# First fixed tiles of three experts take their split weights from SBUF, in 64-row pair products; tile loads cut at 256 rows; another order of the work

## The chip, the cores and the metric

The kernel runs on one core of one Trainium2 chip. The core's engines are named as the profile names them: PE is TensorE (matmuls; PEld is its weight load, which overlaps them), DVE is VectorE, ACT is ScalarE, POOL is GpSimd and SP is SyncE, which here issues nearly all DMA transfers. The metric is the time of one execution on the device in microseconds (us), as the median of several runs; less is better.

## The reference

Eight sequences of 3584 tokens with 192 features go through a causal convolution over seven tokens, whose taps are a softmax per token and head (eight heads of 24 features). Each of the 28672 results then goes to the one expert of eight with the highest gate logit: a relu layer of 1024 features and a layer back to 192, times the gate probability and a sigmoid.

```python
def _attn_ref(x, weight_gen):                      # x (8, 3584, 192), weight_gen (8, 3584, 8, 7)
    w = np.exp(weight_gen - np.max(weight_gen, axis=-1, keepdims=True))
    w = w / (np.sum(w, axis=-1, keepdims=True) + 1e-09)
    x_pad = np.concatenate([np.zeros((B, K - 1, D), dtype=np.float32), x], axis=1)
    idx = np.arange(S)[:, None] + np.arange(K)[None, :]
    x_unf = x_pad[:, idx, :].reshape(B, S, K, H, group)
    return np.einsum('bshk,bskhg->bshg', w, x_unf).reshape(B, S, D)

def _moe_ref(x, w_gate, w_output_gate, w1, w2):    # x (28672, 192)
    logits = x @ w_gate
    e_idx = np.argmax(logits, axis=1)
    probs = np.exp(logits - logits.max(-1, keepdims=True))
    probs /= probs.sum(-1, keepdims=True) + 1e-09
    gate_w = probs[np.arange(N), e_idx]
    eom = 1.0 / (1.0 + np.exp(-(x @ w_output_gate)))
    for e in range(E):
        mask = e_idx == e
        h = np.maximum(x[mask] @ w1[e], 0.0)
        out[mask] = gate_w[mask, None] * eom[mask, e, None] * (h @ w2[e])
```

## The kernel before

**Units.** The tokens are worked in 32 units of 896. For each, softmax taps are made and multiplied with shifted rows of x: some products by POOL (`gap`), the others by DVE (`vap`). For units 0 to 6 (`u < PE_U`) PE adds the seven products, as matmuls with an identity; from unit 7 on DVE adds them in PSUM (`acc_steps`). A unit's rows are then split into two 16-bit parts and laid in a row buffer `rt` (three of them, `RT`), turned, put through the gate matmul, ranked by expert, and scattered, sorted by expert, to DRAM (`srtd`) by seven indirect DMAs of POOL. A row buffer is free again when its unit's seven scatters have landed, so unit u+3's split waits for unit u's scatters. Units 0 to 6 are turned on PE (through PSUM and `gt`), the later ones by transposing DMAs that SP issues.

**Weights.** `weight_steps` stages each expert's w1 and w2 in SBUF (`st`), and `split_steps` scales them (by the sum of squares that ACT takes first) and splits them into high and low 16-bit halves, `wa` for w1 and `wpb` for w2. SP stores both to DRAM (`wd`), and the buffers go back to the pool.

**Tiles.** A tile is up to 512 rows of one expert. `plan_rounds` says how many tiles of which size are made after which unit. After unit 2 come eight fixed tiles of 256 rows, one per expert (`EACH`, made by `each_table`); later rounds choose the experts with the most waiting rows (`round_table`), and the last round takes the rest. For a tile, SP loads its rows' gate values (`meta`), its rows with a transposing DMA (`xT` or `xTb`, two buffers in turn), and its weights (`wa`, `wb`) from `wd`; `tile_steps` keeps two tiles ahead (`AHEAD`, `LATE`). The rows have 192 features in two parts, so three blocks of 128 partitions; the middle one holds 64 rows of each part. ACT copies its first 64 rows to a tile `dup` whose other half is zero (`twin_steps`). The first layer, `gemm1_unit`, then makes five products per 128 features of the hidden layer: three with blocks 0 and 2, and two with the middle block and `dup`. `gemm1_twins` is another form, for up to four tiles of the last round that are 128 rows long: there products of 64 rows stand in pairs on the two halves of the array. ACT takes relu (`hh`), DVE the low part (`hl`), PE makes the second layer (`gemm2_group`, 24 products per 128 rows), ACT scales it (`ys`), and POOL scatters it to the output by an indirect DMA.

**What sets the order.** All five engines' instructions are recorded by a planner (`Order`, `Chain`, `Paced`, `Queue`) before the kernel is built. Each chain of steps has a rank (`RANK_*`, with exceptions in `RK` and `FAVOUR`); the planner has a cost for each operation and due times (`FIRST` for the start, `LATER` after it, `PACKET` and `TURN_NS` for DMAs), and at each step it takes the chain that may go first. An engine runs its list in order: an instruction that waits holds up all behind it. In the profile almost every operation therefore has the same line (165, or 140 for SP), and groups are told apart by their tiles' names. PSUM banks for tiles are given by `bank_steps`, not before unit 6 has been split:

```python
yield T_, lambda: (len(ahead) >= GIVE or "split" in U[PE_U - 1]) and any(f[1] == 0 for f in sum_free)
```

## Time and profile before

| what | value |
|---|---|
| median of three runs | 1207.81 us (1205.61 to 1212.14) |
| the profiled execution's own time | 1206.35 us |
| its span in the profile | 1204.6 us |
| PE busy | 1108.7 us, 92% of the span |
| DVE busy | 930.3 us, 77% |
| POOL busy | 833.3 us, 69% |
| ACT busy | 653.6 us, 54% |
| mean busy share of the 16 DMA engines, main queue | 68.2% |
| HBM | 174.87 MB read, 59.62 MB written |

The profile is of one execution. Its page gives the busy time of each engine; the views of its trace cut that by stretches of time, by tile and operation, by what an engine waited for, or show each operation in order of time. The idle time of an engine matters only where the end of the kernel hangs on it.

### The profile page before, as it was taken

Reading aid. Unit: us, or ns where it says so; the run is one execution under the profiler, and the core shown is the slowest. Engines: PE = TensorE matmul, PEld = TensorE weight load, DVE = VectorE, ACT = ScalarE, POOL = GpSimd, SP = SyncE. Lnnn points to the kernel's source line nnn. Section 1 sums busy time; section 2 is a strip of 40 time slices with the busy share of each in tenths; the row PEclk is TensorE's granted clock in tenths of the full one; section 3 lists DMA queues with packets and bytes.
Section 4 is the critical chain, followed back from the end, with each engine's and each line's share of the span. In section 5 each row is a group of like instructions: output and inputs, shape, how many; then the busy total and the mean of one; then the engine's idle time right before and its main releaser. Section 6 shows DMA issues by size and latency. Waiting matters only on the chain.

```text
span 1204.6 us, 27077 instructions
## 1 busy us (share of the span) xinstructions
PE 1108.7 (92%) x9707; PEld 806.5 (67%) x9707; DVE 930.3 (77%) x1776; ACT 653.6 (54%) x1418; POOL 833.3 (69%) x613
## 2 busy tenths in 40 slices
...
GB/s 275 189 215 222 267 245 270 248 255 288 250 240 179 253 228 179 197 280 207 188 259 238 214 220 157 237 219 187 214 204 209 159 208 288 286 215 336 279 302 44
DMA packets 269129, 275.56 MB, mean 229 GB/s; under 512 B 206918, under 2 KB 231479, under 8 KB 267968
## 3 DMA queue, kind: packets, MB, share of 16 engines
q1 hardware_dynamic: 247152, 229.21, 68.2%
...
HBM read 174.87 MB, written 59.62 MB: 195 GB/s over the span
## 4 chain that ended last, share of the span: by engine, by line
PE 40%; DVE 23%; DMA 16%; issue 8%; POOL 5%; SPq 5%; ACT 3%; DVEq 0%; POOLq 0%; ACTq 0%
PE ps L165 40%; DVE ps L165 11%; DMA srtd<-rt,posi 6%; SPq L140 5%; DVE hl L165 3%; DMA xTb<-srtd 3%; DMA xs<-in_x_dram 2%; DVE hlb L165 2%; POOL gap L165 2%; DVE vt L165 2%; DMA xT<-srtd 2%; POOL out_dram L165 2%; DVE rt L165 1%; POOL srtd L165 1%; DMA wa<-wd 1%
## 5 line engine op out<-in xcount | busy, mean ns | idle before, releaser
L165 POOL TENSOR_TENSOR gap<-xs,w 128x1344 f32<-128x1344 f32 x145 | 376.7, 2602 | 51.7 <-DVE ps L165 21.5
L165 PEld LDWEIGHTS <-wa 128*128 128x128 f16 (+1 forms) x2440 | 227.3, 98 | 205.4 <-issue 25.6
L165 POOL DMA_INDIRECT out_dram<-ys,meta x216 | 214.7, 994 | 211.6 <-ACT ys L165 165.4
L165 POOL DMA_INDIRECT srtd<-rt,posi x224 | 226.1, 1009 | 92.5 <-issue 59.8
L165 PE MATMUL ps<-wb,hh 128*128 128x192 f16 x1888 | 243.1, 246 | 3.4 <-ACT ys L165 2.7
L165 PE MATMUL ps<-xT,wa 128*128 128x512 f16 (+3 forms) x1056 | 224.5, 343 | 19.3 <-DMA wa<-wd 6.6
L165 PE MATMUL ps<-wb,hl 128*128 128x192 f16 x944 | 232.2, 246 | 0.0
L165 PE MATMUL ps<-wb,hhb 128*128 128x192 f16 x1760 | 227.5, 246 | 1.3 <-DVE hl L165 0.8
L165 DVE SCALAR_TENSOR_TENSOR hl<-ps,hh 128x512 f16<-128x512 f32 (+1 forms) x240 | 158.1, 672 | 83.6 <-ACT hh L165 83.2
L165 PE MATMUL ps<-wb,hlb 128*128 128x192 f16 x880 | 216.7, 246 | 0.0
L165 DVE SCALAR_TENSOR_TENSOR hlb<-ps,hhb 128x512 f16<-128x512 f32 (+1 forms) x226 | 146.6, 666 | 84.8 <-ACT hhb L165 84.3
L165 PE MATMUL ps<-xTb,wa 128*128 128x512 f16 (+3 forms) x928 | 203.6, 349 | 8.1 <-DMA wa<-wd 3.1
L165 ACT ACTIVATE ys<-ps,sc 128x192 f32<-128x192 f32 x228 | 96.0, 421 | 182.2 <-PE ps L165 115.9
L165 ACT ACTIVATE hh<-ps 128x512 f16<-128x512 f32 (+1 forms) x240 | 139.4, 589 | 88.2 <-PE ps L165 85.3
L165 PEld LDWEIGHTS <-hh 128*128 128x128 f16 x1888 | 170.9, 98 | 21.7 <-issue 4.2
L165 DVE TENSOR_TENSOR ps<-ps,gap 128x1344 f32<-128x1344 f32 x117 | 181.2, 1549 | 1.8 <-POOL gap L165 1.5
L165 PEld LDWEIGHTS <-hhb 128*128 128x128 f16 x1760 | 159.8, 98 | 20.7 <-issue 2.9
L165 ACT ACTIVATE hhb<-ps 128x512 f16<-128x512 f32 (+1 forms) x226 | 129.5, 585 | 77.2 <-PE ps L165 75.9
L165 PE MATMUL ps<-dup,wa 128*128 128x512 f16 (+5 forms) x456 | 155.9, 352 | 0.0
L165 PEld LDWEIGHTS <-hl 128*128 128x128 f16 x944 | 92.3, 98 | 0.0
L165 PEld LDWEIGHTS <-hlb 128*128 128x128 f16 x880 | 86.2, 98 | 0.0
L165 PE MATMUL ps<-gap,cf 128*128 128x512 f32 x168 | 73.9, 581 | 13.3 <-POOL gap L165 11.7
...
## 6 DMA issues: line engine op xcount, KB each, us to landing
...
```

Source lines behind the costliest of these rows:

```text
L140: r = f(*args, **kwargs)
L165: r = f(*args, **kwargs)
```

## The change

- **Weights where they lie.** For experts 5, 6 and 7 (`DIRECT`) the split halves `wa` and `wpb` stay in SBUF after they have been stored; the first fixed tile of each uses them, and its load reads only `meta` and rows. These buffers go back to the pool after that tile. Every other tile of these experts loads its weights as before.
- **Pair products.** In `wa` as it was split, the middle block's weights lie on both halves of the partitions (the first 512 hidden features on one, the others on the other). For the three tiles, `swap_steps` copies both halves of the middle block crosswise into a new tile `swap` (two buffers of 256 columns), and `gemm1_direct` makes the block's products as 64-row products in pairs, one on each half of the array: 24 of these beside 24 full ones.
- **Loads.** A tile's transposing load is cut at 256 rows (`TSPLIT`).
- **Copies.** The plan counts the copy to `dup` as possible 3.7 us later than the transposing load's end (`DUP_LAG`).
- **Order.** The fixed tiles come in the order 5, 6, 7, 0 to 4 (`EACH_ORDER`). `EARLY`, and with it the sizes of the rounds, changes: the round of unit 5 has one tile of 512 rows (before three of 384), that of unit 6 four of 384 (two), that of unit 7 none (one of 512), that of unit 8 two of 512 (one). In all there are 14 tiles of 256 rows, 4 of 384, 43 of 512 and 16 of 128 (before 13, 5, 43 and 15). `each_table` has tiles of its own per unit. `RK`, `FAVOUR`, `RANK_T` and the planner's costs have other numbers.

The numbers of products per engine for the sums of units 0 to 6 (`FRONT`, `PAIRS`) are written anew in the diff but come out as before; these lines are left out below.

```diff
@@ -247,7 +247,7 @@
 def sync_issue(name, args, kwargs):
-    return 1.2 if name == "dma_start_transpose" else 0.532
+    return 1.3 if name == "dma_start_transpose" else 0.532
@@ -274,6 +274,8 @@
     run = size * min(run_of(o), run_of(kwargs["in_"]))
+    if run == 4 * WA_W:
+        return n / run * 300.0 / 16e3
@@ -465,7 +467,8 @@
         dup_free.append(dup)
-    state = {"base": base, "writers": [], "t": 0, "weights": 0, "rounds": 0, "rows": 0, "stored": {}}
+    swap_free = [cp.tile([P, 256], F16, name=f"swap{i}") for i in range(2)]
+    state = {"base": base, "writers": [], "t": 0, "weights": 0, "rounds": 0, "rows": 0, "stored": {}, "here": {}, "used": set()}
@@ -601,7 +604,8 @@
         od.cur.t = max(od.cur.t, SP.moved + 1.0)
-        wa_free.append((od.cur.t, wa))
+        if e not in DIRECT:
+            wa_free.append((od.cur.t, wa))
@@ -611,9 +615,12 @@
         st_free.append(od.cur.t)
+        if e in DIRECT:
+            state["here"][e] = (od.cur.t, wa, wb)
...
         SP.dma_start(out=wd[e, :, WA_W:WW], in_=wb)
-        wb_free.append((od.cur.t, "wb"))
+        if e not in DIRECT:
+            wb_free.append((od.cur.t, "wb"))
@@ -1008,7 +1015,7 @@
         state["step"] = None
-        ge, to, ti = (sp.tile([1, NE], d, tag=k, bufs=1, name=f"{k}{u}") for k, d in (("ege", F32), ("eto", F32), ("eti", I32)))
+        ge, to, ti = (sp.tile([1, NE], d, tag=f"{k}{u}", bufs=1, name=f"{k}{u}") for k, d in (("ege", F32), ("eto", F32), ("eti", I32)))
@@ -1077,15 +1084,20 @@
+    def direct(e):
+        return e in DIRECT and e not in state["used"]
...
         while "all" not in state or queue:
-            yield SP, lambda: queue and dup_free and (state["weights"] == NE or queue[0][4] in state["stored"]) and len(ahead) < (LATE if "all" in state else AHEAD)
+            yield SP, lambda: queue and (direct(queue[0][4]) and swap_free or not direct(queue[0][4]) and dup_free and (state["weights"] == NE or queue[0][4] in state["stored"])) and len(ahead) < (LATE if "all" in state else AHEAD)
             _, xT = yield from take(xt_free, SP)
-            _, ka = yield from take(wa_free, SP)
-            _, kb = yield from take(wb_free, SP)
+            ka = kb = None
+            if not direct(queue[0][4]):
+                _, ka = yield from take(wa_free, SP)
+                _, kb = yield from take(wb_free, SP)
             T, ti, i, pads, fixed, ready = queue[0]
-            ready = max(ready, state["stored"].get(fixed, 0.0))
+            ready = max(ready, state["stored"].get(fixed, 0.0) if ka is not None else 0.0)
@@ -1095,6 +1107,8 @@
             d = tile_load(state["t"], T, ti, i, list(state["writers"]), ka, kb, xT, fixed)
+            if ka is None:
+                state["used"].add(fixed)
@@ -1107,13 +1121,19 @@
             e = bass.ds(nc.sync.snap(expert, min_val=0, max_val=NE - 1), 1)
-        else:
+        elif ka is not None:
...
         loaded(SP.dma_start(out=meta[:, 0:Gn, :], in_=rows[:, W - 2 : W].rearrange("(g p) c -> p g c", p=P)), writers)
-        loaded(SP.dma_start_transpose(out=xT[:, :, 0:T], in_=rows.bitcast(F16)[:, 0:384]), writers)
-        turned = od.cur.t
+        for lo in range(0, T, TSPLIT):
+            hi = min(T, lo + TSPLIT)
+            loaded(SP.dma_start_transpose(out=xT[:, :, lo:hi], in_=srtd[bass.ds(row + lo if lo else row, hi - lo), :].bitcast(F16)[:, 0:384]), writers)
+        turned = od.cur.t + DUP_LAG
+        if ka is None:
+            d = dict(t=t, T=T, G=Gn, units=8 // (512 // T), meta=meta, xT=xT, own=own, hh={}, hl={}, hl_t=0.0, dup=swap_free.pop(0), twin=None, h=[])
+            od.add(swap_steps(d), (RANK_H,), S, turned)
+            return d
@@ -1124,6 +1144,40 @@
         return d
+    def swap_steps(d):
+        xT, T = d["xT"], d["T"]
+        S.copy(d["dup"][64:128, 0:T], xT[0:64, 1, 0:T])
+        S.copy(d["dup"][0:64, 0:T], xT[64:128, 1, 0:T])
+        yield S, lambda: d["own"] in state["here"]
+        ready, ka, wb = state["here"].pop(d["own"])
+        d.update(ka=ka, kb="wb", wa=ka.bitcast(F16), wb=wb.bitcast(F16), inv=wb.bitcast(F32)[:, 1536:1537])
+        d["dup_t"] = max(od.cur.t, ready)
+    def gemm1_direct(d, u, banks):
+        T, wa, xT, dup = d["T"], d["wa"], d["xT"], d["dup"]
+        nf = 512 // T
+        us = [u + k * d["units"] // 2 for k in range(2)]
+        hs = d["h"][-2:]
+        def place(k, i):
+            return ps[:, banks[k] + i * T : banks[k] + (i + 1) * T]
+        for i in range(nf):
+            for q in range(3):
+                for k in range(2):
+                    p0, at = 64 * k, 2048 + (u * nf + i) * P + (512 if q == 2 else 0)
+                    rhs = xT[p0 : p0 + 64, 1, 0:T] if (q == 1) == (k == 1) else dup[p0 : p0 + 64, 0:T]
+                    T_.matmul(place(k, i), lhsT=wa[p0 : p0 + 64, at : at + P], rhs=rhs, start=(i == 0 and q == 0), stop=False, skip_group_check=True)
+        for k, at in enumerate(banks):
+            _, hh, hl = hs[k]
+            for i in range(nf):
+                f = (us[k] * nf + i) * P
+                for q, (wo, b) in enumerate(((f, 0), (1024 + f, 0), (f, 2))):
+                    T_.matmul(place(k, i), lhsT=wa[:, wo : wo + P], rhs=xT[:, b, 0:T], start=False, stop=(q == 2), skip_group_check=True)
+            od.add(evac_steps(d, ps[:, at : at + nf * T], hh[:, 0 : nf * T], hl[:, 0 : nf * T], at, us[k]), (RANK_H,), S, T_.t + od.m("LAT_P"), ("h", d["t"], us[k]))
@@ -1277,7 +1331,18 @@
                 moved = True
-            elif cur is not None and cur["twin"] is None and len(h_free) >= 2:
+            elif cur is not None and "own" in cur and len(h_free) >= 2:
+                yield T_, lambda: "dup_t" in cur
+                banks = []
+                for _ in range(2):
+                    _, at = yield from take(bank_free, T_)
+                    cur["h"].append((yield from take(h_free, T_)))
+                    banks.append(at)
+                od.cur.t = max(od.cur.t, cur["ready"], cur["dup_t"])
+                gemm1_direct(cur, i // 2, banks)
+                i += 2
+                moved = True
+            elif cur is not None and cur["twin"] is None and "own" not in cur and len(h_free) >= 2:
@@ -1290,7 +1355,7 @@
                     wa_free.append((od.cur.t, cur["ka"]))
-                    dup_free.append(cur["dup"])
+                    (swap_free if "own" in cur else dup_free).append(cur["dup"])
@@ -1401,17 +1466,20 @@
 RANK_S = 1.5
-RANK_T = 5
-TURN_NS = 30.0
+RANK_T = 3.5
+TURN_NS = 27.0
+TSPLIT = 256
+DUP_LAG = 3.7
...
-LATER = {'LAT': 0.125, 'LAT_S': 0.037, 'LAT_G': 0.04, 'LAT_P': 0.167, 'LAT_T': 2.466, 'LAT_R': 0.0, 'LOCK': True, 'SLACK': 0.0, 'LEAD': 5.44, 'WBX': 5.724}
-CONST_AT = 4.2
+LATER = {'LAT': 0.112, 'LAT_G': 0.009, 'LAT_P': 0.084, 'LAT_R': 0.0, 'LAT_S': 0.037, 'LAT_T': 2.401, 'LEAD': 5.44, 'LOCK': True, 'SLACK': 0.0, 'WBX': 5.724}
+CONST_AT = 2.2
 STG = 2
+DIRECT = (5, 6, 7)
@@ -1429,13 +1497,13 @@
 PRO_G = 4
...
-RK = {('b', 0): 1.2, ('b', 1): 1.5, ('b', 2): 1.2, ('b', 7): 5.5, ('c', 0): 1.2, ('c', 1): 1.2, ('e', 1): 1.2, ('e', 6): 4.8, ('g', 5): 1.5, ('l', 1): 4.2, ('l', 6): 1.5, ('r', 2): 1.2, ('r', 9): 4.8, ('s', 2): 1.5, ('x', 0): 6.5, ('x', 8): 6.5}
+RK = {('a', 9): 1.5, ('b', 4): 1.5, ('b', 9): 2.2, ('c', 4): 2.2, ('c', 5): 4.2, ('c', 7): 1.5, ('e', 4): 1.5, ('e', 6): 3.5, ('e', 8): 2.8, ('g', 4): 4.2, ('l', 2): 4.8, ('l', 3): 2.2, ('r', 9): 2.2, ('v', 0): 4.2, ('x', 8): 4.8, ('x', 9): 4.8}
...
 SHARES = {}
-FAVOUR = {('e', 8): -1.6, ('s', 1): 4.1}
+FAVOUR = {('e', 5): -1.4, ('h', 1, 0): 1.2, ('s', 1): 4.1, ('y', 2, 1): -2.6}
@@ -1443,12 +1511,13 @@
 DEFER = 6
...
 EACH = {2: (256,)}
-EACH_ORDER = tuple(range(8))
-EARLY = {2: ((256, 0),), 3: ((512, 0),), 5: ((384, 0),), 6: ((384, 0),)}
+EACH_ORDER = (5, 6, 7, 0, 1, 2, 3, 4)
+EARLY = {2: ((384, 0),), 3: ((384, 0),), 4: ((512, 0),), 6: ((384, 0),)}
```

How the lists of the engines move is shown at three places. Numbers behind a name tell buffers apart; the first number of `gap`, `posi` and `vap` is the unit.

POOL before, around the scatters of unit 3 (`posi3`), whose last one gives row buffer `rt_0` back for unit 6:

```order
L165 TENSOR_TENSOR gap6_3_1182<-xs1_84,w6_672 128x1344
L165 DMA srtd_78<-rt_0_99,posi3_1137 262144x194 x3
L165 TENSOR_TENSOR gap7_0_1241<-xs1_84,w7_849 128x1344
L165 DMA srtd_78<-rt_0_99,posi3_1137 262144x194
L165 TENSOR_TENSOR gap7_1_1266<-xs1_84,w7_849 128x1344
L165 DMA srtd_78<-rt_0_99,posi3_1137 262144x194
L165 TENSOR_TENSOR gap7_2_1315<-xs1_84,w7_849 128x1344
L165 DMA srtd_78<-rt_0_99,posi3_1137 262144x194 x2
L165 DMA srtd_78<-rt_1_100,posi4_1329 262144x194 x7
```

POOL after, at the same place:

```order
L165 TENSOR_TENSOR gap6_2_1244<-xs1_84,w6_746 128x1344
L165 DMA srtd_78<-rt_0_99,posi3_1124 262144x194 x2
L165 TENSOR_TENSOR gap6_3_1305<-xs1_84,w6_746 128x1344
L165 DMA srtd_78<-rt_0_99,posi3_1124 262144x194
L165 DMA srtd_78<-rt_1_100,posi4_1313 262144x194
L165 DMA srtd_78<-rt_0_99,posi3_1124 262144x194
L165 DMA srtd_78<-rt_1_100,posi4_1313 262144x194
L165 DMA srtd_78<-rt_0_99,posi3_1124 262144x194
L165 DMA srtd_78<-rt_1_100,posi4_1313 262144x194
L165 TENSOR_TENSOR gap7_0_1420<-xs1_84,w7_860 128x1344
```

The products of unit 7 (`gap7`) stood among the last scatters of unit 3; now they stand behind them, and scatters of unit 4 have come between unit 3's last three.

SP before, around the loads of the tiles numbered 1 and 2 (`meta1`, `xT1`, `meta2`); `wa0`, `wa1`, `wpb6` are the split weights of experts on their way to DRAM:

```order
L140 DMA meta1_1384<-srtd_78 128x2x2
L140 ISA
L140 DMA_TRANSPOSE xT1_168<-srtd_78 128x3x256
L140 DMA wa2_138<-wd_79 128x1536
L140 DMA wb1_1388<-wd_79 128x1537
L140 DMA wd_79<-wa1_137 128x1024
L140 DMA wd_79<-wa1_137 64x256 x4
L140 DMA wd_79<-wpb6_1479 128x1537
L140 TENSOR_LOAD eti2_877
L140 ISA x3
L140 DMA meta2_1606<-srtd_78 128x2x2
L140 ISA
```

SP after, around the load of tile 2:

```order
L140 DMA wd_79<-wa0_136 128x1024
L140 DMA wd_79<-wa0_136 64x256 x4
L140 DMA wd_79<-wpb6_1394 128x1537
L140 DMA wd_79<-wa1_137 128x1024
L140 DMA wd_79<-wa1_137 64x256 x4
L140 DMA wd_79<-wpb7_1523 128x1537
L140 TENSOR_LOAD eti2_850
L140 ISA x3
L140 DMA meta2_1650<-srtd_78 128x2x2
L140 ISA
L140 DMA_TRANSPOSE xTb0_1614<-srtd_78 128x3x256
L140 TENSOR_LOAD eti2_850
```

The load of tile 2 has no load of weights behind it now, and stands behind the stores of the last two experts' weights, where before only one store stood ahead of it; tile 1's load has gone further ahead.

DVE before, ahead of the split of unit 6 (the last row, `rt`); `cs`, `nx`, `z`, `ge`, `ti` belong to the table of a round:

```order
L165 SCALAR_TENSOR_TENSOR cs_127<-gg5_0_1433,ps_82 1x24
L165 TENSOR_REDUCE ps_82<-w9_1243 128x56
L165 SCALAR_TENSOR_TENSOR z5_0_1429<-cs_127,nx5_0_1428 1x8x3
L165 TENSOR_TENSOR ge5_0_1452<-cs_127,ps_82 1x27
L165 TENSOR_SCALAR ps_82<-ps_82 128x56
L165 SCALAR_TENSOR_TENSOR ps_82<-cs_127,z5_0_1429 1x8
L165 TENSOR_TENSOR ge5_0_1452<-ge5_0_1452,z5_0_1429 1x27
L165 RECIPROCAL ps_82<-ps_82 128x56
L165 TENSOR_REDUCE ti5_0_1461<-ge5_0_1452 1x3
L165 TENSOR_TENSOR w9_1243<-w9_1243,ps_82 128x56x5
L165 SCALAR_TENSOR_TENSOR rt_0_99<-ps_82,sx6_1435,rt_0_99 128x7x192
```

DVE after, ahead of the same split:

```order
L165 SCALAR_TENSOR_TENSOR ps_82<-cs_127,ps_82 1x8
L165 TENSOR_TENSOR ge5_0_1432<-ge5_0_1432,ps_82 1x9
L165 TENSOR_REDUCE ps_82<-lz5_1376 128x7
L165 TENSOR_TENSOR w9_1338<-w9_1338,ps_82 128x392
L165 TENSOR_REDUCE ti5_0_1444<-ge5_0_1432 1x1
L165 TENSOR_SCALAR ps_82<-ps_82 128x2
L165 TENSOR_SCALAR wsc7_1446<-ps_82 128x2
L165 TENSOR_SCALAR winv7_1447<-ps_82 128x2
L165 TENSOR_SCALAR ex_x6_1461<-ssq6_1439 128x1
L165 SCALAR_TENSOR_TENSOR ez5_1454<-ps_82,ez5_1454 128x7
L165 RECIPROCAL ez5_1454<-ez5_1454 128x7
L165 SCALAR_TENSOR_TENSOR rt_0_99<-ps_82,sx6_1459,rt_0_99 128x7x192
```

The table of unit 5's round is one of three tiles before (24 numbers, with `z` in SBUF) and of one tile after (8 numbers, with its result in PSUM); the scaling of the weights of expert 7 (`wsc7`) and the factors of unit 6 (`ex_x6`) stand ahead of the split now.

## Rows read from the trace of the kernel before

**Rows 1.** The page, busy time of each engine with its share and count of instructions

```profile
PE 1108.7 (92%) x9707; PEld 806.5 (67%) x9707; DVE 930.3 (77%) x1776; ACT 653.6 (54%) x1418; POOL 833.3 (69%) x613
```

**Rows 2.** Stretches: length, busy PE, PEld, DVE, ACT, POOL; PE's clock, DMA share, GB/s

```profile
161.00:180.00 19.00, 2.88 (x25) 2.67 (x25) 14.24 (x27) 8.46 (x17) 10.53 (x8) 0.50 0.64 205
180.00:260.00 80.00, 72.28 (x735) 64.91 (x734) 67.46 (x100) 46.62 (x103) 47.62 (x29) 0.95 0.93 260
260.00:980.00 720.00, 687.62 (x6038) 492.15 (x6036) 650.00 (x1274) 406.11 (x930) 582.42 (x429) 1.00 0.81 218
1100.00:1204.60 104.60, 96.82 (x1114) 82.17 (x1112) 30.43 (x44) 44.60 (x97) 24.48 (x25) 0.97 0.76 230
```

**Rows 3.** Waits of PE, by releaser: us in total, times, longest us

```profile
PE ps L165 <- DMA wa<-wd: 9.7, 6, 2.8
PE ps L165 <- ACT ys L165: 9.0, 10, 1.9
PE ps L165 <- DVE hl L165: 6.7, 12, 1.2
PE ps L165 <- DVE hlb L165: 6.2, 10, 2.2
```

**Rows 4.** Timeline, 145 to 181 us: start, us, engine, operation [idle before <- releaser]

```profile
145.69 1.48 ACT L165 ACTIVATE wa<-st 128x1536 bf16<-128x1536 f32 x1
...
157.99 0.98 POOL L165 DMA_INDIRECT srtd<-rt,posi  x1 [0.31 <-issue]
...
164.86 0.22 ACT L165 ACTIVATE rt<-tok 128x14 int32<-128x14 f32 x1 [6.06 <-DMA srtd<-rt,posi]
...
167.72 5.40 DVE L165 SCALAR_TENSOR_TENSOR z<-cs,nx 1x24 f32<-1x24 f32 x1
...
167.98 5.10 POOL L165 TENSOR_TENSOR gap<-xs,w 128x1344 f32<-128x1344 f32 x2
...
176.33 2.40 PE L165 MATMUL ps<-ident,rt 128*128 128x128 f16 x21 [14.94 <-DVE rt L165]
...
179.72 1.01 PE L165 MATMUL ps<-xT,wa 128*128 128x256 f16 x4 [0.99 <-ACT gt L165]
...
180.15 1.01 POOL L165 DMA_INDIRECT srtd<-rt,posi  x1 [7.08 <-ACT rt L165]
```

**Rows 5.** Timeline of SP's queue: the first load of tiles 2, 5 (rows), 14

```profile
185.33 0.42 SPq L140 DMA_DIRECT2D meta<-srtd  x1
...
219.77 1.25 SPq L140 DMA_TRANSPOSE xTb<-srtd  x1
...
321.79 0.39 SPq L140 DMA_DIRECT2D meta<-srtd  x1
```

**Rows 6.** Waits of all engines: ACT's copies, for one pair of buffers

```profile
ACT dup L165 <- DMA xTb<-srtd: 41.6, 22, 4.0
```

**Rows 7.** Timeline of PE, pair products of a tile of the last round

```profile
1053.93 0.38 PE L165 MATMUL ps<-dup,wa 64*128 64x512 f16 x1
1054.23 2.98 PE L165 MATMUL ps<-xTb,wa 128*128 128x512 f16 x13
```

**Rows 8.** Timelines of POOL, PE, DVE; then two groups by line (busy, mean ns)

```profile
191.51 1.01 POOL L165 DMA_INDIRECT srtd<-rt,posi  x1 [0.17 <-issue]
...
195.88 0.60 PE L165 MATMUL ps<-xT,wa 128*128 128x256 f16 x4
...
196.42 0.60 PE L165 MATMUL ps<-xT,wa 128*128 128x256 f16 x4
...
288.76 0.26 DVE L165 TENSOR_TENSOR_SCAN p<-segs,ps 128x56 f16<-128x56 f16 x1
...
320.48 1.03 PE L165 MATMUL ps<-xTb,wa 128*128 128x512 f16 x4
...
L165 DVE SCALAR_TENSOR_TENSOR hl<-ps,hh 128x512 f16<-128x512 f32 (+1 forms) x240 | 158.1, 672 | 83.6 <-ACT hh L165 83.2
...
L165 DVE TENSOR_TENSOR ps<-ps,gap 128x1344 f32<-128x1344 f32 x117 | 181.2, 1549 | 1.8 <-POOL gap L165 1.5
```

13 lines of the change are left out of this document (7 added, 6 removed).

## The prediction, made before the changed kernel had run

> **What bounds the kernel now.** I read the page's busy line first: TensorE (PE) is busy 1108.7 of 1204.6 us [rows 1], so it idles 95.9 us in all. The reader is to see that no other engine comes near that, and that a gain must be idle time of PE, or PE work, that goes away. The work hardly changes: the plan gives tiles of 512, 384, 256 and 128 rows in the numbers 43, 5, 13, 15 before and 43, 4, 14, 16 after, 29184 rows both times. So I read PE's idle time by stretch, as length less PE busy [rows 2]: 16.1 us in 161 to 180, 7.7 in 180 to 260, 32.4 in the 720 us from 260 to 980 and 7.8 after 1100; the rest, some 32 us, lies mostly before 161. Next the waits of PE [rows 3] say what ends those after the start: weights (wa) 9.7 us, ys 9.0, hl and hlb together 12.9. Last the timeline around the one large gap [rows 4], where the first tile is held.
>
> That gap reads as a chain. Unit 6 may not be split before unit 3's last scatter gives back its row buffer (there are three); ScalarE (ACT) waits 6.06 us for it until 164.86. Then VectorE (DVE) should finish the split (rt) at once, but ahead of it z, an operation on 24 numbers, takes 5.40 us, from 167.72, while GpSimd (POOL) runs two products, 167.98 to 173.08. PE waits 14.94 us for rt, turns unit 6 at 176.33 and begins tile 0 at 179.72. Tile 0 had been loaded long before: the first tile is held by unit 6, not by its rows or weights. The PSUM banks for tiles come free with that split (`bank_steps`).
>
> **The change part by part.** The sum stands against the profiled execution's own time, 1206.35 us (span 1204.6 and 1.75 around it); the median of the three runs, 1207.81, is 1.5 above.
>
> *Order at the start: -7.* POOL now has three products fewer and two scatters more ahead of unit 3's last scatter. At 2.55 us a product (5.10 for two) and about 1.3 a scatter (0.98 and the gap to the next) that is 7.7 - 2.6 = 5.1 us earlier: 164.86 becomes about 159.8. The round of unit 5 has one tile instead of three, and with one the table's z lies in PSUM, so the 5.40 us row is gone from ahead of the split: about 5 more. Against it, ACT now takes the two squares of the last expert's staged weights ahead of unit 6's: two of some 1.5 us [rows 4], 3.0. So tile 0 starts about 5.1 + 5 - 3 = 7 us earlier, at 172.5. Bounds: nothing, and the whole 16.1 of the gap. Unit 6's fourth product stands a few scatters later on POOL; the cover is that it still stands ahead of unit 3's last scatters, for which the split waits anyway, and without that cover it would cost its 2.55. What is late next is tile 2, in the rivals below.
>
> By the row, z is free of its wait if no product of POOL runs beside it. The Trainium skill, SBUF — State Buffer, section SBUF: two separate sides, calls the port pair that VectorE and GpSimd share an exclusive lock, held for a whole instruction, which a VectorE operation with two SBUF inputs must have. Unit 6's round has four tiles now, so a z with two SBUF inputs comes some 30 us later; by the page it can be shut out again, for up to the 5.1 us of two products, and the sum would be 5 worse; by the rows alone it is a chance and I take nothing.
>
> *Weights used where they lie: -2.* Tiles 0 to 2 (experts 5, 6, 7) no longer read 1536.5 KB each back; 4.6 MB at the 260 GB/s of 180 to 260 [rows 2] is 17.7 us of a DMA that is 93% busy there. PE's waits for weights are 9.7 us in six [rows 3]; I take 2 of them. Bounds: 0 and -5. The three buffers are held longer, but tile 3's weights need only tile 0's buffer, which frees after its first products.
>
> *Pair products: -0.3.* A normal 256-row tile has 40 products of 256 columns, five of them in the 0.54 us from 195.88 to 196.42 [rows 8], 0.108 each: 4.32 us. The new form has 24 full ones and 24 half-array ones in 12 pairs, 36 places, 3.89. The nearest row for pairs is the paired form of the last tiles [rows 7]: from the last pair at 1053.93 to the next full product at 1054.23 are 0.30 us, where 512 columns take 0.216, so a change of form costs 0.084. Four changes are 0.34, which leaves 0.09 a tile, 0.3 for three. Bounds: -1.3 (no cost of a change) and +1. The Trainium skill, TensorEngine Tiling (Array Packing), section Tiling Modes, says that a change of tiling mode drains the engine and promises up to a doubling for halves; by the promise alone the sum would have -1.3 here, and the row sides with the drain. The second copy of the swapped half is one more short operation of ACT for a tile, beside other work.
>
> *Later copies: -3.* In ACT's order the copy of a tile's third feature block stands too early: it waits 41.6 us for the loads of one pair of buffers in 22 pieces [rows 6], and with it the evacuations queued behind on ACT, then DVE, then PE, whose hl, hlb and ys waits are 21.9 us in all [rows 3]. The change puts each copy 3.7 us later in the plan. Bounds: 0 and -21.9. I take 3, near the low end, since PE's list has other ready work in most of those waits.
>
> *Loads of at most 256 rows: 0.* 47 tiles get two transposing loads. One of 256 rows takes SP 1.25 us [rows 5], so each such tile costs SP at most 1.25 us more and its weights are issued that much later. The cover is the lead of loads: tile 2's was issued at 185.33 and its first product ran at 195.88 [rows 5, 8]. Without the cover it is 1 us for a tile; bounds 0 and +5. What queues behind on SP are the next unit's row transposes and loads of x.
>
> *Last round: +1.* One more tile of 128 rows and one more of 256 for one of 512 means one more read of about 1.66 MB at the end. PE idles 7.8 us after 1100 [rows 2]; bounds 0 and +6.
>
> *Order of the middle: 0.* In DVE's order unit 7's rank scan has 24 evacuations and 17 sums ahead of it, where it had 36 and 25; unit 8's has 37 and 25 where it had 52 and 31. At 0.67 and 1.55 us (the means of the two groups) [rows 8] and one split less that is about 22 and 21 us. It is needed: unit 7 now has no tile, so tile 13 takes unit 8's rows. It starts 140.8 us after tile 0 (320.48 less 179.72), and by 128 rows more ahead, some 5 later (1108.7 us for 29184 rows is 4.9 for 128): at about 318. Unit 8's tile load came 33 us after its scan (288.76 and 321.79) [rows 5, 8]; 21 earlier is about 301. So it is covered, by 17 us; without the new order, at 322, PE would wait about 4 and the load's own time there.
>
> The sum: -7 - 2 - 0.3 - 3 + 0 + 1 + 0 = -11.3, and 1206.35 - 11.3 = 1195.
>
> **The rivals.** *Slower: tile 2 behind unit 5's scatter.* Its load now stands on SP behind the stores of the last two experts and waits for 39 scatters, all of units 0 to 4 and four of unit 5. If those run as now, the fourth starts at 191.51 and ends at 192.5. A scatter lands some 6 us later (the one of 157.99 ends at 158.97, and ACT is released at 164.86 [rows 4]), and the load takes some 5 (an estimate: tile 2's took 10.6 from issue to first product, its turn behind tile 1 in it). So tile 2 starts at 203.5 instead of 195.88 [rows 8]: +7.6, and the earlier gains are spent waiting. With the last round, 1206.35 + 7.6 + 1 - 0.3 = 1215. For it: the wait is there. Against it: in POOL's new order that scatter has two products fewer and four scatters more ahead than the one at 180.15 had, which itself waited 7.08 us on ACT [rows 4] and no longer would; I reckon it at 176, its landing at 182, and tile 2's need at 172.5 + 16.2 = 188.7. It decides once the fourth scatter starts after about 181.
>
> *Given back in the middle.* Tiles can't run ahead of the units that feed them. If units 9 to 12 come no earlier than now, PE, 7 us ahead, waits for rows, and only the copies and pairs are left: 1206.35 - 3 - 0.3 + 1 = 1204. For it: later units lead by only 6 to 13 us of DVE work in the new order, and unit 12's first tile is due 12 us sooner. Against it: that lead is there at all.
>
> *More than that.* The whole gap goes (-16.1), and 10 of the 21.9 us behind the copies: 1206.35 - 16.1 - 2 - 0.3 - 10 + 1 = 1179.
>
> **How the numbers follow.** Forecast 1195 with its own range of 1187 to 1202: 0.53. Given back, 1204: 0.20. Slower, 1215: 0.14. More, 1179: 0.13. About 0.5% (6 us) is what a measurement of this kernel tells from no change, so faster is below 1201.8 and slower above 1213.8. Faster holds the forecast but for 0.03, the larger gain, and 0.03 of given back: 0.66. Slower holds 0.10 of its rival; the rest, 0.24, is within. The range of 1183 to 1212 leaves out about 0.07 below and 0.11 above; the bounds of the loads and of the last round lie in it.
>
> **What would show it.** Right: in the timeline, tile 0's first product near 172, no z of 5 us ahead of unit 6's split, tile 2 within 17 us of tile 0; in the waits, ACT's for xTb well under 41.6 us; PE's idle time in 161 to 260 near 15 instead of 23.8. Wrong: PE waiting between tiles 1 and 2, tile 13 waiting for its load, idle time in 260 to 980 above the 32.4 us of now, or more than 8 us after 1100. The step I trust least is the middle: hundreds of instructions moved there and I cost them at nothing.

## The result, and the profile after

The changed kernel takes 1188.83 us, the median of four runs (1182.54 to 1193.68); the kernel before, run with it, 1206.71 us. The ratio is 0.984, with an interval of 0.980 to 0.987: 1.6% faster. The profiled execution took 1191.02 us, with a span of 1189.2. The forecast was 1195, its range 1183 to 1212. Two executions behind the numbers below, each some 1.5% above the fastest of its kernel, are left out of the ratios.

The page's busy line, beside [rows 1]:

```profile
PE 1108.4 (93%) x9771; PEld 809.5 (68%) x9771; DVE 926.5 (78%) x1766; ACT 656.5 (55%) x1421; POOL 836.2 (70%) x613
```

PE is as busy as before (1108.7). Its idle time fell from 95.9 to 80.8 us, and that is the whole gain. The same stretches as in [rows 2], and the stretch from 980 to the end, which was not shown of before (columns as there), first of after:

```profile
161.00:180.00 19.00, 9.71 (x92) 7.45 (x94) 16.57 (x25) 12.12 (x22) 15.83 (x10) 0.55 0.42 151
180.00:260.00 80.00, 73.88 (x767) 63.49 (x766) 72.07 (x129) 46.33 (x110) 53.18 (x33) 0.98 0.92 237
260.00:980.00 720.00, 700.80 (x6138) 504.65 (x6139) 649.40 (x1267) 410.64 (x928) 587.40 (x435) 0.99 0.86 222
980.00:1189.20 209.20, 191.72 (x2204) 163.61 (x2201) 61.10 (x89) 86.67 (x188) 58.67 (x60) 0.98 0.83 249
1100.00:1189.20 89.20, 77.15 (x933) 68.32 (x931) 23.50 (x34) 35.28 (x79) 21.29 (x22) 0.98 0.73 223
```

and the last stretch of before:

```profile
980.00:1204.60 224.60, 214.03 (x2344) 175.85 (x2342) 73.14 (x126) 97.70 (x206) 70.50 (x72) 0.99 0.82 247
```

Length less PE busy, before and after:

| stretch | before | after | difference | the terms of the prediction there |
|---|---|---|---|---|
| up to 161 (the rest of the idle time) | 29.1 | 28.7 | -0.4 | none |
| 161 to 260 | 23.8 | 15.4 | -8.4 | -7 (order at the start) -2 (weights) -0.3 (pairs) |
| 260 to 980 | 32.4 | 19.2 | -13.2 | -3 (copies), 0 (loads), 0 (order of the middle) |
| 980 to the end | 10.6 | 17.5 | +6.9 | +1 (last round) |

The start came out as forecast; the middle gave four times what the forecast had, and the end took more than half of the surplus back.

**The start.** Timelines of after, in the order of the chain of [rows 4] (start, duration, engine, operation, idle before and its releaser):

```profile
153.05 0.98 POOL L165 DMA_INDIRECT srtd<-rt,posi  x1 [0.30 <-issue]
...
160.38 0.22 ACT L165 ACTIVATE rt<-tok 128x14 int32<-128x14 f32 x1 [5.03 <-DMA srtd<-rt,posi]
...
161.21 0.15 DVE L165 SCALAR_TENSOR_TENSOR ps<-cs,ps 1x8 f32<-1x8 f32 x1
...
165.33 1.62 DVE L165 SCALAR_TENSOR_TENSOR rt<-ps,sx,rt 128x1344 f16<-128x1344 f32 x1 [1.90 <-ACT rt L165]
...
167.00 2.40 PE L165 MATMUL ps<-ident,rt 128*128 128x128 f16 x21 [11.10 <-DVE rt L165]
170.40 0.37 PE L165 MATMUL ps<-xT,wa 64*128 64x256 f16 x1 [0.99 <-ACT gt L165]
173.06 0.40 PE L165 MATMUL ps<-swap,wa 64*128 64x256 f16 x2 [2.29 <-ACT gt L165]
```

Unit 3's last scatter starts 4.9 us earlier (157.99 before; 5.1 was forecast). The table of unit 5's round has no z of 5.40 us any more, but operations of 0.15 us in PSUM. Unit 6 is turned 9.3 us earlier (176.33 before) and tile 0 begins at 170.40 instead of 179.72, though its second product waits 2.29 us more: the pair form (`gemm1_direct`) takes two PSUM banks at once, and the second one comes free with ACT's second copy of `gt`, which ends at 173.01. Tile 2 begins at 188.30 instead of 195.88.

**The copies.** ACT's waits for the tiles' rows, beside the one of [rows 6]; then PE's waits, beside [rows 3] (total, times, longest):

```profile
ACT dup L165 <- DMA xT<-srtd: 6.4, 7, 1.6
ACT dup L165 <- DMA xTb<-srtd: 3.7, 4, 1.8
```

```profile
PE ps L165 <- DMA twin<-wd: 7.0, 4, 3.1
PE ps L165 <- DMA wa<-wd: 6.6, 2, 3.5
...
PE ps L165 <- DVE hl L165: 5.8, 5, 1.6
...
PE ps L165 <- DVE hlb L165: 3.4, 4, 1.4
PE ps L165 <- ACT dup L165: 2.6, 2, 1.6
```

The wait of 41.6 us for xTb is 3.7 now, and no wait of PE for ys is left (9.0 before). The waits for twin are those of the last round's tiles.

**The middle.** The rank scans of DVE, one for each unit; these rows are those of units 8 and 9:

```profile
258.26 0.27 DVE L165 TENSOR_TENSOR_SCAN p<-segs,ps 128x56 f16<-128x56 f16 x1
289.66 0.26 DVE L165 TENSOR_TENSOR_SCAN p<-segs,ps 128x56 f16<-128x56 f16 x1
```

Unit 8's scan is 30 us earlier (288.76 in [rows 8]), and the units now follow each other every 29 to 32 us (unit 10 at 318.53, unit 11 at 349.60). The lead does not hold behind it: units 9 and 10 are only 8 and 12 us ahead of before (297.91 and 330.77 there).

### The profile page after: what moved, and what is told of

It is laid out like the page before. It is cut to its first block, busy times and chain, and to the rows that moved or that the text cites. A ratio compares the mean times of both kernels' runs of the same rounds, so it can differ in the third digit from the quotient of the medians.

```text
span 1189.2 us, 27329 instructions
## 1 busy us (share of the span) xinstructions
PE 1108.4 (93%) x9771; PEld 809.5 (68%) x9771; DVE 926.5 (78%) x1766; ACT 656.5 (55%) x1421; POOL 836.2 (70%) x613
## 4 chain that ended last, share of the span: by engine, by line
PE 50%; DVE 17%; DMA 12%; issue 10%; POOL 6%; SPq 3%; ACT 2%; POOLq 0%; DVEq 0%; ACTq 0%
PE ps L165 50%; DVE ps L165 7%; DMA w<-in_wg_dram 3%; POOL out_dram L165 3%; SPq L140 3%; DMA srtd<-rt,posi 2%; POOL gap L165 2%; POOL srtd L165 2%; DMA out_dram<-ys,meta 2%; DVE hlb L165 2%; DVE hl L165 1%; DMA wa<-wd 1%; DVE vt L165 1%; DVE rt L165 1%; DMA xs<-in_x_dram 1%
## 5 line engine op out<-in xcount | busy, mean ns | idle before, releaser
L165 PEld LDWEIGHTS <-wa 128*128 128x128 f16 (+1 forms) x2428 | 221.1, 99 | 186.3 <-issue 18.4
L165 PE MATMUL ps<-wb,hh 128*128 128x192 f16 x1760 | 228.3, 247 | 1.6 <-DVE hl L165 1.6
L165 DVE SCALAR_TENSOR_TENSOR hlb<-ps,hhb 128x512 f16<-128x512 f32 (+1 forms) x232 | 152.2, 671 | 94.7 <-ACT hhb L165 94.3
L165 PE MATMUL ps<-wb,hl 128*128 128x192 f16 x880 | 217.1, 247 | 0.0
L165 PE MATMUL ps<-xTb,wa 128*128 128x512 f16 (+4 forms) x964 | 208.3, 347 | 9.2 <-DMA wa<-wd 3.5
L165 PE MATMUL ps<-xT,wa 128*128 128x512 f16 (+4 forms) x1000 | 210.0, 341 | 5.9 <-DMA wa<-wd 3.2
L165 DVE SCALAR_TENSOR_TENSOR hl<-ps,hh 128x512 f16<-128x512 f32 (+1 forms) x232 | 152.0, 671 | 73.1 <-ACT hh L165 72.9
L165 ACT ACTIVATE hhb<-ps 128x512 f16<-128x512 f32 (+1 forms) x232 | 135.2, 588 | 98.5 <-PE ps L165 96.8
L165 PEld LDWEIGHTS <-hhb 128*128 128x128 f16 x1824 | 165.7, 98 | 19.7 <-issue 1.8
L165 PE MATMUL ps<-dup,wa 128*128 128x512 f16 (+4 forms) x428 | 147.6, 355 | 0.0
```

Of the source, the lines that this page charges most:

```text
L165: r = f(*args, **kwargs)
```

## The experiments

The theory after this comparison was that the gain has three sources, each acting on a stretch of its own: the start by the z and by POOL's order, the middle by the later copies, with something given back at the end. The rival was that the new order (sizes or ranks) carries the middle too, and that ACT's waits were slack. Each kernel below undoes one part of the change, or does one part alone. The three groups of four ran on three chips, on which the kernel before takes 1207, 1203 and 1246 us; so kernels are compared by their ratio to the kernel before in the same group. The changed kernel itself was measured twice in this way, at 0.984 and 0.987, so a difference from it that goes over two groups is known to some 4 us only.

### One part alone: the sizes of the rounds

```diff
 # the kernel before
-EARLY = {2: ((256, 0),), 3: ((512, 0),), 5: ((384, 0),), 6: ((384, 0),)}
+EARLY = {2: ((384, 0),), 3: ((384, 0),), 4: ((512, 0),), 6: ((384, 0),)}
```

> The kernel before with the new sizes of the rounds (EARLY) alone. The round of unit 5 has one tile, so no z of 24 numbers stands ahead of unit 6's split. Theory (the gain has three sources: the start by the z and by POOL's order, the middle by the later copies, and the end gives some back): no row of 5 us ahead of unit 6's split, tile 0 some 5 us earlier than 179.7, PE idle in 260 to 980 still near the 32 us of before, 5 to 7 us more idle at the end; together 1201 to 1208. Rival (the new sizes carry the middle's gain): idle in 260 to 980 below 25 us and a time of 1190 to 1197.

Measured: 1207.94 us, ratio 1.000 (0.998 to 1.002): the upper end of the theory's range, and not the rival's time. Its stretches 180 to 260 and 260 to 980, and one wait of PE between 170 and 320:

```profile
180.00:260.00 80.00, 66.06 (x666) 59.31 (x664) 67.05 (x95) 43.44 (x95) 47.33 (x27) 0.94 0.89 253
260.00:980.00 720.00, 693.77 (x6084) 496.20 (x6083) 656.41 (x1295) 406.66 (x932) 586.86 (x436) 1.00 0.80 218
```

```profile
PE ps L165 <- DMA wa<-wd: 10.8, 1, 10.8
```

The z is gone and tile 0 starts at 175.10, 4.6 us earlier, as the term said. But PE then idles 13.9 us instead of 7.7 between 180 and 260, mostly in one wait of 10.8 us for the weights of tile 4. SP issued that tile's load at 213.80, after it had waited 6.7 us for scatters and 2.9 for a store of weights. What the start won was spent there; of the rest, 6 us less in the middle (26.2) were given back after 980 (16.9 against 10.6).

### One part alone: the later copies

```diff
 # the kernel before, tile_load
-        turned = od.cur.t
+        turned = od.cur.t + 3.7
```

> The kernel before with the copies to dup put 3.7 us later in the plan, and nothing else. Theory: ACT's waits for the tiles' rows fall from 73 us to below 20, PE's waits for ys from 9 to below 3 and PE's idle time in 260 to 980 from 32 to below 24; the time is 8 to 12 us below before, 1195 to 1199. Rival (the waits of ACT are slack): ACT's waits go, PE's idle time in 260 to 980 stays above 29, and the time is within 3 us of before.

Measured: 1196.26 us, ratio 0.990 (0.987 to 0.993), some 11 to 12 us less, as the theory had it. ACT's two waits for rows fall to 5.8 and 1.2 us, PE's waits for ys to 3.6 (the theory had less than 3), and PE idles 19.1 us in the middle instead of 32.4, as little as in the changed kernel (19.2):

```profile
260.00:980.00 720.00, 700.86 (x6175) 505.12 (x6174) 660.95 (x1310) 415.40 (x945) 594.61 (x441) 1.00 0.82 223
```

This run also shows why an operation on 24 numbers can take 5 us. The z takes 0.17 us here, but now another operation of the same table, gg, stands beside the two products of POOL:

```profile
167.54 5.51 DVE L165 SCALAR_TENSOR_TENSOR gg<-base,nx 1x24 f32<-1x24 f32 x1
...
167.90 5.10 POOL L165 TENSOR_TENSOR gap<-xs,w 128x1344 f32<-128x1344 f32 x2
```

Both of gg's inputs lie in SBUF here, and it ends at 173.05, just after POOL's products (173.00). In the changed kernel the gg of the four-tile table took 1.01 us, from 198.48 to 199.49, where POOL's products ended at 199.44. The lock described by the Trainium skill, SBUF — State Buffer, section SBUF: two separate sides, fits all three: by that rule it is not this one row that is slow, but any DVE operation with two SBUF inputs that comes while POOL multiplies.

The trace of before bears that out beyond these rows. Eighteen DVE operations with two SBUF inputs, of those that the timeline shows one by one, overlap a product of POOL. Twelve of them end behind it, by a time that goes with their length: 0.02 to 0.06 us (8 to 32 numbers a partition), 0.54 to 0.56 (512), 1.08 to 1.09 (1024), 1.63 (1536). Of the other six, five end 2.41 to 2.43 us ahead of the product's end and one 4.94 ahead of the end of two, nearly whole products (2.57 each), so there POOL waited. In the next kernel the z of the same table comes late in a product and takes 0.51 us, ending 0.05 behind it. Which of the two engines was first can't be read from the starts: gg begins 0.36 us before POOL's products here and still ends behind both.

### One part alone: the ranks and the planner's costs

```diff
 # the kernel before, with these of the changed kernel:
-RANK_T = 5
-TURN_NS = 30.0
+RANK_T = 3.5
+TURN_NS = 27.0
...
-CONST_AT = 4.2
+CONST_AT = 2.2
...
-FAVOUR = {('e', 8): -1.6, ('s', 1): 4.1}
+FAVOUR = {('e', 5): -1.4, ('h', 1, 0): 1.2, ('s', 1): 4.1, ('y', 2, 1): -2.6}
```

and RK, LATER and `sync_issue` in the same way. The changed kernel's own cost for one form of DMA (in `sync_cost`) is not in this edit.

> The kernel before with the new ranks and planner's costs alone (RK, FAVOUR, RANK_T, TURN_NS, LATER, CONST_AT and the two DMA costs). POOL has 29 instead of 31 products ahead of unit 3's last scatter; the z stays ahead of unit 6's split. Theory: tile 0 comes 2 to 5 us earlier, the middle as before (idle 29 to 35 us in 260 to 980), and the time is 1202 to 1207. Rival (the new ranks carry the middle's gain): idle in 260 to 980 below 25 us, time 1190 to 1197.

Measured: 1200.05 us, ratio 0.992 (0.989 to 0.995), 2 us below the theory's range and above the rival's, with a course that neither had. Tile 0 starts at 168.09, 11.6 us earlier, where 2 to 5 were expected: z still stands ahead of the split, but takes 0.51 us. PE then idles 11.5 us between 180 and 260 (7.7 before) and 30.3 in the middle, so the ranks don't carry the middle's gain.

### One part undone: the later copies

```diff
 # the changed kernel
-DUP_LAG = 3.7
+DUP_LAG = 0.0
```

> The changed kernel with the copies at their old place in the plan (DUP_LAG 0). Theory: ACT's waits for the tiles' rows are back above 50 us, PE's waits for ys back at 5 us or more, PE's idle time in 260 to 980 at 27 to 32 instead of 19; the time is 8 to 12 us above the changed kernel, 1197 to 1201. Rival (the waits of ACT are slack): the time stays at 1186 to 1192 with ACT's waits back.

Measured: 1219.21 us, ratio 1.009 (1.006 to 1.012): 27 to 30 us above the changed kernel by the ratios, and slower than the kernel before. The direction is the theory's, the size some three times as large. PE idles 45.6 us in the middle:

```profile
260.00:980.00 720.00, 674.43 (x5891) 482.08 (x5892) 635.89 (x1210) 390.69 (x897) 568.38 (x417) 0.99 0.81 212
```

One place shows how a copy that stands too early costs PE. Timeline of SP, ACT and PE, 404 to 413 us:

```profile
404.77 2.59 SPq L140 DMA_TRANSPOSE xT<-srtd  x2
...
411.17 0.62 ACT L165 COPY dup<-xT 64x512 f16<-64x512 f16 x1 [6.11 <-DMA xT<-srtd]
...
412.25 0.40 ACT L165 ACTIVATE ys<-ps,sc 128x192 f32<-128x192 f32 x1
...
412.70 1.41 PE L165 MATMUL ps<-xT,wa 128*128 128x512 f16 x4 [2.99 <-ACT ys L165]
```

The load is issued at 404.77, and its rows are there 6.4 us later. ACT waits for them 6.11 us, with an evacuation (ys) of the tile at work behind the copy; PE waits 2.99 us for the bank that ys gives free. PE's waits in 260 to 980 tell how the 26 us more of idle time are made up; first of this kernel, then the changed kernel's wait for p (p is a unit's rank scan):

```profile
PE ps L165 <- DVE p L165: 15.4, 15, 3.2
PE ps L165 <- ACT ys L165: 7.9, 5, 3.0
PE ps L165 <- DVE hl L165: 7.4, 11, 1.2
PE ps L165 <- DMA wa<-wd: 7.3, 2, 6.2
PE ps L165 <- DVE hlb L165: 7.2, 12, 1.0
```

```profile
PE ps L165 <- DVE p L165: 8.0, 8, 2.9
```

In the changed kernel the others are 0 (ys), 5.8 (hl), 3.2 (wa) and 3.4 (hlb). So 13 of the 26 us are waits for what stands behind ACT's copies (ys, hl, hlb), 7 are waits for the ranks of units, and 4 for weights. The rest of the distance between the two profiled executions is mainly 8 us more of PE busy time for the same number of products.

How the copies make the ranks and the weights later is not settled. A split needs ACT for a part of its work, and SP's list holds the units' row transposes and the tiles' loads in one order, so a loop could be read: while ACT waits for a tile's rows the split is late, SP waits for the split, and the next tile's load stands behind that. SP's waits in 260 to 980 don't bear it out as it stands:

| kernel | copies | SP's wait for a unit's split | SP's wait for scatters | PE idle, 260 to 980 |
|---|---|---|---|---|
| before | old place | 101.0 | 101.7 | 32.4 |
| sizes alone | old place | 65.9 | 126.1 | 26.2 |
| ranks alone | old place | 137.2 | 78.8 | 30.3 |
| this kernel | old place | 100.3 | 96.2 | 45.6 |
| copies alone | later | 67.9 | 157.3 | 19.1 |
| changed kernel | later | 35.5 | 144.2 | 19.2 |

With the copies later the wait for splits is shorter than in most of the others, but the sizes alone, with the copies at their old place, have as little of it as the copies alone; and where it falls, the wait for scatters grows. No run broke the loop at another place than the copies.

### One part undone: the weights where they lie

```diff
 # the changed kernel
-DIRECT = (5, 6, 7)
+DIRECT = ()
...
-EACH_ORDER = (5, 6, 7, 0, 1, 2, 3, 4)
+EACH_ORDER = tuple(range(8))
```

> The changed kernel without the use of weights where they lie, and with the fixed tiles in the order 0 to 7 again. First theory (the term of the prediction: 2 us, bandwidth of three reads): tiles 3 to 8 at their times within 3 us, the time at 1190 to 1193. Second theory (formed from the runs so far, where the new sizes alone and the copies alone won nothing by tile 13 because PE waited 9 to 11 us once for the weights of the first tile of expert 5, 6 or 7, which SP stores last): tile 0 still near 170, one wait of PE for wa of 7 to 11 us between 200 and 235, tile 13 some 7 us later than 317, and a time of 1194 to 1200.

Measured: 1205.44 us, ratio 1.001 (0.998 to 1.003): undoing this part takes the whole gain away. That is beyond the second theory's time too, whose wait for weights is there. (The edit also gives the three tiles the old form of products and puts the fixed tiles back in order 0 to 7.) PE idles 21.2 us between 180 and 260, instead of 6.1; 13.0 us of it are waits for weights. Timelines of SP and PE in this kernel:

```profile
197.64 3.27 SPq L140 DMA_DIRECT2D wd<-wa  x5
205.55 9.90 SPq L140 DMA_TRANSPOSE gt<-rt  x7
...
217.05 0.42 SPq L140 DMA_DIRECT2D meta<-srtd  x1
...
220.17 0.38 SPq L140 DMA_DIRECT2D wd<-wpb  x1
...
225.10 1.03 PE L165 MATMUL ps<-xT,wa 128*128 128x256 f16 x4 [7.40 <-DMA wa<-wd]
```

and of SP in the changed kernel, the last store of weights and the load of tile 2 (rows only):

```profile
177.09 0.34 SPq L140 DMA_DIRECT2D wd<-wpb  x1
181.20 0.41 SPq L140 DMA_DIRECT2D meta<-srtd  x1
```

There are three buffers for `wa`. A fixed tile that reads its weights back takes one of them while the last experts' weights are still to be split. Without the direct use the last split weights are stored at 220.17, with it at 177.09 (before: 206.51). On SP the store of the last `wa` (197.64), and unit 7's seven row transposes, stand ahead of the load of tile 4 (217.05), for which PE waits 7.40 us; in the changed kernel the same tile's load is issued at 195.66, ahead of those transposes (204.05).

The late splits cost PE in a second way, which no expectation had. Timelines of DVE, POOL and PE:

```profile
188.74 6.59 DVE L165 SCALAR_TENSOR_TENSOR wa<-st,wsc,wa 128x512 f16<-128x512 f32 x1
...
187.17 7.61 POOL L165 TENSOR_TENSOR gap<-xs,w 128x1344 f32<-128x1344 f32 x3
...
195.99 1.01 PE L165 MATMUL ps<-xT,wa 128*128 128x256 f16 x4 [5.84 <-DVE hl L165]
```

This piece of a split, which takes 0.74 us in the changed kernel (169.53, no product of POOL beside it), ends 0.55 us behind POOL's three products. The evacuation hl stands behind it on DVE, and PE waits 5.84 us for that. These two waits are 13.2 of the 15.1 us that PE idles more here. So what the direct use brings is that the splits are done earlier; it is not the bandwidth of three reads (the DMA share from 180 to 260 is 0.82 here and 0.92 in the changed kernel). That the buffers are what held the splits is read from the kernel and these lists: no run had a fourth buffer. How much of the loss goes with the pair form and the order of the fixed tiles was not separated, and a part of it is where POOL's products happened to fall. This is its price in the new order; what it would bring to the old order alone was not run.

### One part undone: loads of at most 256 rows

```diff
 # the changed kernel
-TSPLIT = 256
+TSPLIT = 512
```

> The changed kernel with loads of whole tiles again (TSPLIT 512). Theory (the prediction's zero): 1186 to 1192, SP busy less, ACT's waits for the tiles' rows below 15 us. Rival (a shorter load ends sooner, so the copies are on time only with it): ACT's waits for rows above 25 us and a time of 1194 to 1202. Other rival (the second load costs SP): 1182 to 1186.

Measured: 1180.67 us, ratio 0.981 (0.977 to 0.984); ACT's waits for rows stay at 2.8 us in all. The time is below all three that were expected, but the kernel before was 4 us faster on this chip as well; by the ratio it is 0.3% below the changed kernel's first, with intervals that overlap. So it was run again, below.

### One part undone: the sizes of the rounds

```diff
 # the changed kernel
-EARLY = {2: ((384, 0),), 3: ((384, 0),), 4: ((512, 0),), 6: ((384, 0),)}
+EARLY = {2: ((256, 0),), 3: ((512, 0),), 5: ((384, 0),), 6: ((384, 0),)}
```

> The changed kernel with the sizes of the rounds of before. Theory (the sizes win 5 us at the start by taking the z away from ahead of unit 6's split and lose 5 to 7 at the end, with a last round of more tiles): a z of 24 numbers ahead of the split again, tile 0 at 172 to 176, the stretch from the first tile of the last round to the end about 183 us instead of 186, and a time of 1184 to 1191. Rival (the sizes are needed, because a unit's table comes too late without them): PE waits for tile 13 and the time is 1194 or more.

Measured: 1192.84 us, ratio 0.991 (0.988 to 0.995). The start is as the theory had it: gg and z of 24 numbers stand ahead of the split again (2.77 and 2.91 us, each ending behind a product of POOL), and tile 0 begins at 172.18. The theory's range was missed by 2 us. The ratio is above the changed kernel's 0.984 and 0.987, by 9 or 6 us; against the second the intervals overlap, so that the new sizes are worth something beside the other parts is likely and not shown, and alone they bring nothing. PE's idle time, 81.6 us, is hardly above the 80.8 of the changed kernel, whose profiled execution took only 3 us less than this one's: where the rest lies these two traces don't tell.

### More of one part: the copies later still

```diff
 # the changed kernel
-DUP_LAG = 3.7
+DUP_LAG = 6.0
```

> The changed kernel with the copies 6 instead of 3.7 us later in the plan. Theory (what matters is that the copy stands behind the end of its load; at 3.7 it nearly always does): ACT's waits for rows below 6 us, and the time within 5 us of the changed kernel, 1184 to 1194, since a copy too late in turn holds the tile's fifth product. Rival (the later the better): 1178 to 1183.

Measured: 1188.73 us, ratio 0.987 (0.983 to 0.990): no more than at 3.7, as the theory said. PE's waits for the copies themselves rise from 2.6 to 7.2 us. The copy has to stand behind its load's end; in these two runs more is of no use.

### The changed kernel again, the loads, and the last round

```diff
 # the changed kernel, the last round as it was before
-EARLY = {2: ((384, 0),), 3: ((384, 0),), 4: ((512, 0),), 6: ((384, 0),)}
+EARLY = {2: ((384, 0),), 3: ((384, 0),), 4: ((512, 0),), 6: ((384, 0),), 28: ((384, 0),)}
```

Four kernels ran side by side: the changed one, the one with whole loads, the one with this edit, and the one with both.

> The changed kernel as it is, as a measure for the other three on the same chip: ratio to before 0.980 to 0.988.

> The changed kernel with loads of whole tiles once more, now beside the changed kernel on the same chip. If the second load of a tile costs what the first run of this edit suggested, it is 4 to 9 us below the changed kernel; if that was the chip of that day, within 3 us of it.

> The changed kernel with five tiles of 384 rows after unit 28, by which the last round gets the sizes it had before (two of 512, five of 256, five and ten of 128 rows); all lists are the same up to unit 28. Theory (the last round's sizes cost 5 to 7 us): the stretch from the last round's first tile to the end, with 128 rows more in it, is 183 us or less instead of 186.3, and the time 1 to 5 us below the changed kernel, the one weight load more of the 384-row tiles set against it. Rival (the end costs more because PE arrives earlier than the last units' rows and loads, not for its sizes): PE idles 16 us or more after 980 again and the time is the same or above.

> Both edits, loads of whole tiles and the last round of before. Theory: the two add up, as they act on different stretches: 5 to 12 us below the changed kernel, 1177 to 1184. Rival: no more than the better of the two.

Measured, ratios to before: 0.987 (0.983 to 0.991), 0.982 (0.977 to 0.987), 0.985 (0.982 to 0.989) and 0.983 (0.979 to 0.987), in this order. On this chip all kernels are 3% slower, the kernel before too, and PE has a wait that none of the earlier traces of the changed kernel shows (`issue`, 15.1 us in 26 pieces); the ratio of the changed kernel holds.

Whole loads are 0.5% and 0.3% below cut ones here (1223.76 against 1228.74 us, and 1223.02 against 1228.30 with the other edit), and 0.3% in the group before. One pair alone is within the intervals. The two pairs together, put side by side only after the result, are not: the eleven and twelve executions differ by 5.9 us in the mean, with an interval of 2.8 to 8.9. So cutting the loads costs some 6 us on this chip, as the other rival of the first run of that edit had it; by what path is not shown. Both edits together are no better than whole loads alone, which is the rival of the last expectation.

The last round's old sizes do not change the time. Stretches 260 to 980 and from 980 to the end, of the changed kernel and then of the edit, on this chip:

```profile
260.00:980.00 720.00, 670.88 (x5797) 476.90 (x5795) 633.84 (x1199) 390.94 (x895) 573.27 (x419) 0.99 0.80 211
980.00:1232.20 252.20, 234.59 (x2551) 191.50 (x2549) 82.94 (x170) 104.32 (x227) 76.46 (x79) 0.97 0.81 239
```

```profile
260.00:980.00 720.00, 668.52 (x5767) 474.60 (x5768) 635.27 (x1182) 385.17 (x886) 567.14 (x414) 0.99 0.79 209
980.00:1229.90 249.90, 236.12 (x2575) 194.46 (x2572) 86.78 (x182) 109.22 (x243) 79.20 (x81) 0.99 0.82 243
```

With the old sizes PE idles 13.8 us after 980 instead of 17.6, but 51.5 instead of 49.1 ahead of that. The difference there lies between 880 and 980 (8.8 instead of 5.1 us); the first of the five tiles of 384 rows starts at 971.97, and why PE waits more just ahead of them is not shown. The time doesn't change, so neither the theory nor the rival (which had 16 us of idle time or more at the end) is borne out.

That the idle time at the end goes with the sizes of the rounds shows in the other runs as well: after 980 it is 10.6 to 12.8 us in the four kernels with the old sizes (before, the copies alone, the ranks alone, the sizes undone), and 15.4 to 17.5 in five with the new ones (the sizes alone, the changed kernel, and the changed kernel with the copies at their old place, with the copies later still, with whole loads); only without the direct use is it 12.1 with the new sizes.

## Why the prediction was right

The sign, the range and the first stretch were right; the way there was right in part. Point by point:

**Order at the start, -7: right as a sum, by two errors that cancel.** POOL's part was 4.9 us (5.1 forecast) and the z's 5 us went (in the sizes alone 4.6 at tile 0). The subtraction of 3 us for the two squares of ACT was wrong: they stand in ACT's wait for the scatter, which is still 5.03 us long after them, and cost nothing. So the split came 9.3 us earlier; tile 0 lost 2.3 of that again at its second product, for the second bank of the pair form, which the prediction didn't have. That the two nearly cancel is luck. The term counted a z that is gone; the up to 5 us that a later table could lose beside POOL were 1.01 at the gg of the four-tile table, and its z took 0.17. The idle time from 161 to 260, with weights and pairs, is 15.4 us; the text had "near 15".

**Weights where they lie, -2: right as a sum with the start, wrong as a mechanism.** The step priced the reads by bandwidth and PE's waits, and named the held buffers as a cost without effect. What the runs show instead is the time of the last splits: without the direct use the last weights are stored 43 us later (220.17 against 177.09), PE waits 7.4 us for a tile whose load stands behind on SP and 5.8 us for a split that POOL's products held up on DVE, and the kernel loses all of its 1.6%. The new sizes alone fit that in part: a tile 0 that starts earlier only ends in a wait of 10.8 us at tile 4, but there SP had waited for scatters too.

**Pair products, -0.3: nearly nothing.** In tile 2 six pairs take from 188.30 to 189.06, and twelve full products from there to 190.38 (0.110 each):

```profile
188.12 0.25 PE L165 MATMUL ps<-wpb,hl 128*128 128x192 f16 x1
188.30 0.28 PE L165 MATMUL ps<-xTb,wa 64*128 64x256 f16 x1
...
189.06 1.48 PE L165 MATMUL ps<-xTb,wa 128*128 128x256 f16 x12
190.38 0.33 PE L165 MATMUL ps<-wpb,hh 128*128 128x192 f16 x2
```

Six places of 0.108 are 0.65 of the 0.76 us, so the way out of the pair form costs 0.11; the way in, 0.18 us from the product ahead where 192 columns take 0.083 (two products 0.17 us apart), costs 0.10. Four changes are 0.42 us of the 0.43 that a tile saves (0.34 in the prediction). That a change of form drains the engine, as the Trainium skill, TensorEngine Tiling (Array Packing), section Tiling Modes, has it, agrees with these rows, and the doubling of halves is eaten by it at this tile size. The bank that tile 0 waits for, 2.29 us, is a cost of this form too.

**Later copies, -3: the step that failed.** The mechanism was named and its upper end, 21.9, was in the text; I took 3, "since PE's list has other ready work in most of those waits". It was worth 11 to 12 us alone and 27 to 30 beside the other parts. The working counted the waits of PE that end with hl, hlb and ys; they were 21.9 us before and are 9.2 in the changed kernel, so 12.7 us of them, and not 3, were open to the change. It left out the waits for the ranks of units and for weights, which with the copies at their old place make 7 and 4 of the 26 us more in the middle. How a blocked ACT comes to delay those stays open.

**Loads, 0: mis-sized.** Over both pairs on the third chip they cost 5.9 us (2.8 to 8.9), about the step's upper bound of 5; so the cover, the lead of loads, did not hold in full, and where is not shown.

**Last round, +1: mis-sized.** PE idles 6.9 us more after 980, one us beyond the upper bound. PE idles 12.0 us after 1100, where the text had more than 8 as a sign of being wrong. The idle time at the end goes with the sizes of the rounds, but giving the last round its old sizes only moved it to before 980 and didn't change the time, so more reads at the end, as the step had it, are not shown to be the cause. The waits there are for the weights of the pair form (twin, 2.8 us before, 7.0 after) and for the copies (2.6).

**Order of the middle, 0: its cover held.** Tile 13 was loaded at 306.83 (301 in the text) and began at 318.95 (318); unit 8's scan came 30 us earlier, not 21. PE's longest wait in the middle is 3.2 us.

**The rivals.** Tile 2 behind unit 5's scatter did not come: its load was issued at 181.20, where the text had the scatter's landing at 182. It began 17.9 us after tile 0, not within 17. Nothing was given back in the middle; the opposite. The third rival's 10 us from the copies was nearer than the forecast's 3 (13.2 in the middle), but not the whole gap at the start went.

That the sum came out at 1195 against a profiled 1191 rests on two misses of opposite sign, 10 us more gained in the middle and 6 more lost at the end: that is luck. Nor do the parts add up: alone the sizes, the copies and the ranks gave 0, 12 and 10 us, and undoing the copies, the direct weights and the sizes took 27 to 30, 17 to 20 and 6 to 9.
